# Two small edits in the tail of a decode attention kernel: when the last group's sums are scaled, and how one head's wo rows are loaded

## The chip, the cores and the metric

The kernel runs on one core of a Trainium2 chip. The metric is the device time of one execution in microseconds (us), and the median of several runs is compared. A profile comes from one execution of its own, taken by the hardware profiler; its times count from the start of the profiled span.

## What is computed

Two problems A and B of the same shape stand side by side. Each is one decode step of attention over a sliding window, for a batch of 2 and one query position, followed by the output projection:

```python
B, Sq, D = x.shape                     # 2, 1, 576
Hq, Dh = 32, 128                       # 16 key/value heads, two query heads for each
W = min(4096, max(256, Sk // 4))       # 4096 of 16384 positions
q = (x @ wq) as [B, Hq, Sq, Dh]
k, v = the last W positions of k_cache and v_cache, each head repeated twice
p = softmax(q k^T * Dh ** -0.5)
out = (p v) as [B, Sq, Hq * Dh] @ wo   # wo is [4096, 576]
```

The result is A's and B's output side by side. All inputs are bf16.

## The kernel before

**The work and its order.** The caches dominate: for each problem 16 heads and 2 batch entries of 4096 positions of keys and of values. A step of the main loop handles a *slab*: one key/value head pair of both batch entries, 4 MB of keys (K) and then 4 MB of values (V). There are 16 such steps (`ND`), 8 to a problem, numbered 0 to 15; two steps are a *group* `G` (0 to 7), which shares one block of wo rows. A ring of four 4 MB buffers takes the slabs, in an order written out in `stream`: K of a step comes ahead of V of the step before. At the end it is K15, V13, V14, V15. V15 is loaded in two pieces (`PIECES`), three quarters and one quarter of the positions.

**One step.** VectorE (DVE) transposes K in four parts (`do_X`, `L487`), TensorE (PE) multiplies with the queries into PSUM (`do_S`, `L512`, `L169`), DVE takes the maximum (`do_max`, `L522`), which goes through PE, DVE and ScalarE (ACT) into a bias per row (`do_nm`, `do_nm2`, `do_exp`), and ACT takes the exponential (`L557`), whose sums over the positions come out as one column of `rsum`. DVE transposes the probabilities (`do_pC`, `L565`), and PE multiplies them with V in 32 matmuls (`do_PV`, `L601`). ACT copies that accumulator to SBUF (`L613`). For all groups but the last, GpSimd (POOL) then *folds* it: it masks the copy and adds it together in two halvings (`L620`, `L623`, `L628`), into `acc_r`.

**One group.** `do_tot` does two things before: POOL writes `rsel`, the sums in `rsum` times a mask (`L572`, one instruction), and PE multiplies `rsel` by ones (`tot`, `L575`) so that every row has the totals. DVE takes their reciprocal (`do_rsb`, `L585`). PE brings the folded slabs into place (`do_comb`, `L641`; for the last group `L648`), DVE scales them (`do_norm`), PE and ACT redistribute them (`do_redist`, `L699`, `L707`), and PE multiplies with the group's wo rows (`do_proj`, `L734` with `L169`; for the last group `L738`).

**What sets the order.** Every engine runs its own list of operations in the order in which the program adds them; SP's list holds nearly all DMA issues. An operation's dependencies become waits on semaphores: one counter per engine, one semaphore per DMA buffer. The first waits block all that stands behind them on that engine.

**The tail**, after the main loop (lines 834 to 866), is written out by hand. On PE it runs: V13's products in three parts (rounds 0 to 2, 2 to 4, 4 to 8), with the maximum and the bias of step 15 between them; `tot` of the last group; V14's products (PV14); `comb` of 13 and 14; the redistribution; the projection of group 6 (`proj13`, eight heads); V15's first piece; a redistribution; V15's second piece; `comb` of 15; the projection of step 14 (`proj14`, four heads) and that of step 15 (`proj15`, four heads in three parts, `HEADS`). The fold of slab 13 is added to POOL's list when the last part of V13's products is added; in the kernel before, `rsel` of the last group is added after that.

**The wo rows of the last group.** `issue_wo` loads the four heads of step 14 as one transfer. `issue_last` loads those of step 15 as three: the first two heads (288 KB), the third head (144 KB), the fourth head (144 KB), a head being 128 rows of 1152 bytes, one row to a partition. All are issued from SP behind V15's two pieces. Each of the three parts of `proj15` waits for its own transfer.

Of the kernel before, what the change touches and what calls it, by code (L numbers as in the profile page):

```python
# [59 lines left out]
def build_kernel(nc, probs, out, cfg=None):  # L60
# [28 lines left out]
    HH = HD // 2  # L89
# [8 lines left out]
    BIG = -1.0e30  # L98
    PIECES = [(0, 96), (96, 128)]
    HEADS = [(0, 1), (2,), (3,)]  # L100
    NPC = len(PIECES)

    def by_group(G):
# [3 lines left out]
    with es:  # L107
# [53 lines left out]
        wo_sem = [sem("wo%d" % r) for r in range(2)]  # L161
        x_sem = [sem("xload%d" % P) for P in range(NPROB)]
        wl_sem = [sem("wl%d" % n_) for n_ in range(len(HEADS))]
        out_sem = sem("outdone")
        piece_sem = [sem("piece%d" % n_) for n_ in range(NPC)]

# [10 lines left out]
        def dma_op(eng, sem_h, n_dmas, fn, deps, tag):  # L177
            op = S.add(eng, fn, deps, tag)
            dma_count[sem_h] = dma_count.get(sem_h, 0) + 16 * n_dmas
            op.dma = (sem_h, dma_count[sem_h])  # L180
            return op
# [74 lines left out]

        def issue_last(woP, pc, r0, deps):
            for n_, hs in enumerate(HEADS):
                def f(e, n_=n_, hs=hs):
                    t, r = divmod(hs[0], 2)  # L260
                    row = t * HH + r0 + 256 + 128 * r
                    return e.dma_start(wob[:, pc, 4 + hs[0]:4 + hs[0] + len(hs), :],
                                       woP[row:row + 128 * len(hs), :].rearrange("(h d) n -> d h n", d=128)).then_inc(wl_sem[n_], 16)
                wo_last.append(dma_op("sp", wl_sem[n_], 1, f, deps, "wl%d" % n_))

        def issue_wo(G):
            woP = probs[G // GPP][4]
# [50 lines left out]
        def tb_job(fn, tag, deps, which=None):  # L318
            n = tbn[0]
            tbn[0] += 1  # L320
            w = (tb_last[0] + 1) % NTB if which is None else which
            tb_last[0] = w
            bank = TB[w]
            d = list(deps)
            if tb_open[w] is not None:
                d.append(tb_open[w]())
            tb_open[w] = lambda: tb_consumer[n]
            return n, bank, S.add("pe", lambda e: fn(e, bank), d, tag)
# [236 lines left out]
            chain[(s, "pC")] = S.add("dve", lambda e: e.transpose(  # L565
                pC[:, s % NPT, :, :].rearrange("k j c -> k (j c)"), pR[:, :]), d, "pC%d" % s)

        def do_tot(G):
            d = [chain[(2 * G, "exp")], chain[(2 * G + 1, "exp")], init["maskS"]]
            if G >= 1:  # L570
                d.append(chain[(G - 1, "tot")])
            chain[(G, "rsel")] = S.add("pool", lambda e: e.tensor_tensor(  # L572
                rsel[:, :, :], maskS[:].unsqueeze(1).broadcast_to([128, 2, 8]),
                rsum[:].unsqueeze(2).broadcast_to([128, 2, 8]), ALU.mult), d, "rsel%d" % G)
            n, bank, op = tb_job(lambda e, bank: e.matmul(bank[:, 0:16], ones_f[:, :], rsel[:].rearrange("k l c -> k (l c)"),  # L575
                                                          start=True, stop=True), "tot%d" % G, [chain[(G, "rsel")], p_ones_f])
            chain[(G, "tot")] = op
            chain[(G, "tot_n")] = (n, bank)
# [137 lines left out]
        def do_proj(D_):  # L716
            G = D_ // 2
            P = G // GPP
            pc = G % 2
            new = G % GPP == 0  # L720
            if by_group(G):
                parts = [([(Rsb[:, pc, :, s_], s_) for s_ in range(8)], [r_ev[G]], new, True, True)]
            elif D_ < ND - 1:
                parts = [([(Rsb[:, pc, :, s_], s_) for s_ in range(4)], [r_ev[G], wo_dma[G]] + fin_ops, False, False, False)]
            else:
                parts = [([(oTn[:, h, :], 4 + h) for h in hs], [norm[D_], wo_last[n_]], False, False, n_ == len(HEADS) - 1)
                         for n_, hs in enumerate(HEADS)]
            for lhs, deps, start, rstart, rstop in parts:
                def f(e, rest, lhs=lhs, start=start, rstart=rstart, rstop=rstop):
                    last = None  # L730
                    for n_, (l_, s_) in enumerate(lhs):
                        begin, end = n_ == 0, n_ == len(lhs) - 1
                        if by_group(G):
                            first = e.matmul(OT[0:Bb, 0:NB0], l_, wob[:, pc, s_, 0:NB0], start=start and begin, stop=end, skip_group_check=True)  # L734
                            last = matmul_again(e, first, rest[0:Bb, 0:NB1], wob[:, pc, s_, NB0:NOUT], rstart and begin, rstop and end)
                        else:
                            for half in range(2):
                                last = e.matmul(fin(half), l_, wob[:, pc, s_, half * NH:(half + 1) * NH],  # L738
                                                start=False, stop=end, skip_group_check=True)
                    return last  # L740
                deps = deps + [e_ops[(P - 1, 0)]]
                if by_group(G):
                    n, bank, proj[D_] = tb_job(f, "proj%d" % D_, deps)
                    rest_at[G] = bank
                    if G % GPP < GPP - 1 and G < NG - 2:
                        d = [proj[D_]]
                        if new:
                            if P:
                                d.append(e_ops[(P - 1, 1)])
                            rest_add[G] = S.add("dve", lambda e: e.tensor_copy(o_rest[:, :], bank[0:Bb, 0:NB1]), d, "rest%d" % G)  # L750
                        else:
                            d.append(rest_add[G - 1])
                            rest_add[G] = S.add("dve", lambda e: e.tensor_tensor(o_rest[:, :], o_rest[:, :], bank[0:Bb, 0:NB1], ALU.add),  # L753
                                                d, "rest%d" % G)
                        tb_consumer[n] = rest_add[G]
                    elif G == NG - 2:
                        d = [proj[D_], chain[(ND - 2, "exp")], chain[(ND - 2, "max")]]
                        a_ = S.add("act", lambda e: e.activation(fin(0), OT[0:Bb, 0:NH], ACTF.Copy), d, "fin0")
                        tb_consumer[n] = S.add("dve", lambda e: e.tensor_tensor(
                            fin(1)[:, NB0 - NH:NH], o_rest[:, :], bank[0:Bb, 0:NB1], ALU.add), d + [rest_add[G - 1]], "fin1")  # L760
                        fin_ops.append(S.add("dve", lambda e: e.tensor_copy(fin(1)[:, 0:NB0 - NH], OT[0:Bb, NH:NB0]), [a_], "fin2"))
                    else:
                        rest_at[G] = (n, bank)
                else:
                    proj[D_] = S.add("pe", lambda e, f=f: f(e, None), deps, "proj%d" % D_)
# [27 lines left out]
        for s in range(ND):  # L793
            D2 = s - 2
            c = s - 1
            for u in range(NU):
                if c >= 0:
                    if u == 2:
                        do_nm2(c)
                    elif u == 3:  # L800
                        do_exp(c)
                        if c + 2 < ND:
                            do_fill(c + 2)
                do_X(s, u)
                if c >= 0:
                    if u == 0:
                        do_max(c)
                        if c % 2 == 0 and c >= 2:
                            do_rsb(c // 2 - 1)
                    elif u == 3:  # L810
                        do_pC(c)
                if u >= 1:
                    do_S(s, u - 1)
                if u == 1 and s + 1 < ND:
                    do_zq(s + 1)
                if c >= 0 and u == 1:
                    do_nm(c)
                if D2 >= 0 and D2 % 2 == 1 and s < ND - 1:
                    if u == 2:
                        do_comb(D2)  # L820
                        do_norm(D2)
                    elif u == 3:
                        do_redist(D2 // 2)
            do_S(s, NU - 1)
            if D2 >= 0 and D2 % 2 == 1 and s < ND - 1:
                do_proj(D2)
                if D2 == SPP - 1:
                    do_E(0)
            if c >= 0:
                if c % 2 == 1:  # L830
                    do_tot(c // 2)
                if s < ND - 2:
                    do_PV(c, range(NRD), None)
# [5 lines left out]
        do_nm2(s)  # L839
        do_PV(D_, range(2, 4), None)  # L840
        do_exp(s)
        do_pC(s)
        do_PV(D_, range(4, NRD), None)
        do_tot(s // 2)
# [122 lines left out]
```

## Time and profile before

| | |
|---|---|
| median of 3 runs | 365.75 us |
| lowest and highest of them | 364.33, 365.81 us |
| the profiled execution's own time | 366.16 us |
| its span | 364.8 us |
| read from HBM | 153.10 MB, 420 GB/s over the span |
| busy: PE, DVE, ACT, POOL | 63%, 55%, 19%, 10% of the span |
| granted TensorE clock, mean | 0.85 of full speed |

The profiled execution's own time is its span and what lies around it (launch and end). In the views, `L601` is line 601 of the kernel; `x32` counts instructions. A row of the timeline has start, length, engine, line, operation, the tiles written and read, and in brackets the idle time of the engine just before and what ended it. A row of the windows has busy time and instruction count of PE, PE's weight loads, DVE, ACT and POOL, then the granted clock, the mean busy share of the 16 DMA engines, and GB/s.

### The profile page before, as it was taken

The page shows a single profiled execution, that of the slowest core. Times are in us where ns is not written, and L with a number is a line of the kernel's source. Part 1 is how long each engine was busy: PE and PEld are TensorE (multiplying, and loading weights), DVE is VectorE, ACT ScalarE, POOL GpSimd, SP SyncE. Part 2 cuts the span into 40 slices and gives each one's busy share as a digit, 9 for nine tenths or more (in the row PEclk, how much of TensorE's full clock was granted, in tenths as well). Part 3 has the DMA queues.
Part 4 walks back from the last instruction along what each step waited for, and adds up shares of the span by engine and source line. Part 5 has one row for each costly group of instructions (what it writes and reads, how often), then busy time and mean ns, then how long its engine had stood idle before and what let it go on. Part 6 is the DMA issues. An engine that isn't in the chain of part 4 may idle for free.

```text
span 364.8 us, 2762 instructions
## 1 busy us (share of the span) xinstructions
PE 229.9 (63%) x1323; PEld 59.6 (16%) x954; DVE 201.5 (55%) x176; ACT 68.7 (19%) x153; POOL 35.2 (10%) x55
## 2 busy tenths in 40 slices
PE   0398295576756657573885747594763737576757
PEld 0010021112111211111221201111120201111122
DVE  3013698574908375382917567292926658199631
ACT  1046402020300302020300203120210203021311
POOL 1000000004000130004000040003100040200020
PEclk9999589786996968888786988879896978979968
DMA  8999999999999999999999999999999999999993
GB/s 345 446 417 446 417 408 467 402 446 417 416 438 424 446 417 437 435 428 435 413 444 424 442 419 438 435 428 433 406 446 431 431 429 435 438 428 435 416 413 136
DMA packets 7070, 153.25 MB, mean 420 GB/s; under 512 B 778, under 2 KB 1300, under 8 KB 1684
## 3 DMA queue, kind: packets, MB, share of 16 engines
q1 hardware_dynamic: 7052, 153.10, 98.1%
q8 instruction: 8, 0.13, 0.1%
q14 instruction: 2, 0.02, 0.0%
q10 hardware_dynamic: 8, 0.00, 0.0%
HBM read 153.10 MB, written 0.00 MB: 420 GB/s over the span
## 4 chain that ended last, share of the span: by engine, by line
DMA 63%; DVE 17%; PE 17%; ACT 1%; POOL 1%; issue 1%; SPq 0%; DVEq 0%
DMA ring<-in_B_k_cache_dram 34%; DMA ring<-in_A_k_cache_dram 26%; DVE xt L487 15%; PE st L169 6%; PE st L512 4%; DMA x_sb<-in_B_x_dram 3%; PE acc L601 2%; PE st L423 1%; PE ot L734 1%; PE tb L169 1%; DVE nM L535 1%; DVE m L522 1%; PE ot L169 1%; PE tb L423 1%; PE acc L169 1%
## 5 line engine op out<-in xcount | busy, mean ns | idle before, releaser
L487 DVE STREAM_TRANSPOSE xt<-ring 128x2048 f32<-128x2048 f32 x64 | 145.3, 2285 | 76.0 <-DMA ring<-in_B_k_cache_dram 38.8
L512 PE MATMUL st<-xt,zq 128*128 128x512 bf16 x256 | 116.2, 454 | 112.3 <-DVE xt L487 85.9
L169 PE MATMUL st<-xt,zq 128*128 128x512 bf16 x256 | 114.8, 448 | 0.0
L512 PEld LDWEIGHTS st<-xt,zq 128*128 128x128 bf16 x256 | 28.0, 109 | 207.5 <-DVE xt L487 100.6
L601 PE MATMUL acc<-ring,pC 128*32 128x512 bf16 x512 | 37.4, 408 | 0.0
L540 ACT ACTIVATE nMrep<-nM 1x128 f32<-1x128 f32 x16 | 4.9, 308 | 139.7 <-DVE nM L535 139.7
L613 ACT ACTIVATE acc_sb<-acc 128x512 bf16<-128x512 f32 x16 | 9.5, 596 | 86.6 <-PE acc L601 86.6
L565 DVE STREAM_TRANSPOSE pC<-pR 128x1024 bf16<-128x1024 bf16 x16 | 19.4, 1216 | 4.3 <-ACT pR L557 2.1
L620 POOL TENSOR_TENSOR acc_sb<-acc_sb,maskJ 128x1024 bf16<-128x1024 bf16 (+1 forms) x8 | 13.4, 1679 | 79.3 <-ACT acc_sb L613 79.3
L522 DVE TENSOR_REDUCE m<-st 128x1 f32<-128x1024 f32 x16 | 19.0, 1189 | 1.4 <-PE st L169 1.4
L474 POOL TENSOR_TENSOR zq<-qk,maskA 128x128 bf16<-128x128 bf16 x16 | 6.3, 399 | 125.0 <-PE st L169 103.5
L734 PE MATMUL ot<-wob,Rsb 128*2 128x512 bf16 x56 | 18.0, 439 | 0.3 <-ACT Rsb L707 0.3
L557 ACT ACTIVATE pR<-st,bias_sb 128x1024 bf16<-128x1024 f32 x16 | 17.8, 1114 | 0.5
L447 DVE STREAM_TRANSPOSE qtr<-qrow 128x512 f32<-128x512 f32 x8 | 5.7, 711 | 21.0 <-ACT qrow L437 13.6
L388 ACT ACTIVATE st<-maskB 128x1024 f32<-128x1024 bf16 x16 | 16.5, 1031 | 1.6 <-POOL rsel L572 0.4
L601 PEld LDWEIGHTS acc<-ring,pC 128*32 128x32 bf16 x512 | 13.7, 100 | 14.5 <-issue 4.4
L572 POOL TENSOR_TENSOR rsel<-maskS,rsum 128x16 f32<-128x16 bf16 x8 | 1.7, 216 | 106.9 <-ACT pR L557 106.9
L169 PE MATMUL tb<-wob,Rsb 128*2 128x64 bf16 x56 | 11.7, 209 | 0.0
L355 PE MATMUL tb<-ident_b,x_sb 4*128 4x4 bf16 x4 | 0.3, 174 | 14.2 <-DVE x_dup L362 14.2
L753 DVE TENSOR_TENSOR o_rest<-o_rest,tb 2x64 f32<-2x64 f32 x3 | 0.6, 209 | 15.4 <-PE tb L169 15.4
L623 POOL TENSOR_TENSOR acc_sb<-acc_sb 128x512 bf16<-128x512 bf16 (+1 forms) x8 | 8.2, 1030 | 0.6
L734 PEld LDWEIGHTS ot<-wob,Rsb 128*2 128x2 bf16 x56 | 5.3, 95 | 16.0 <-issue 14.4
(83 smaller groups left out, 107.7 us busy)
## 6 DMA issues: line engine op xcount, KB each, us to landing
ring<-in_A_k_cache_dram SPq DMA_DIRECT2D x8, 4096.0 KB, 31.2
ring<-in_A_v_cache_dram SPq DMA_DIRECT2D x8, 4096.0 KB, 32.4
ring<-in_B_k_cache_dram SPq DMA_DIRECT2D x8, 4096.0 KB, 30.7
ring<-in_B_v_cache_dram SPq DMA_DIRECT2D x7, 4096.0 KB, 32.6
wob<-in_A_wo_dram SPq DMA_DIRECT2D x4, 1152.0 KB, 33.5
ring<-in_A_wq_dram SPq DMA_DIRECT2D x1, 4096.0 KB, 12.6
ring<-in_B_wq_dram SPq DMA_DIRECT2D x1, 4096.0 KB, 22.4
wob<-in_B_wo_dram SPq DMA_DIRECT2D x3, 1152.0 KB, 33.6
```

What stands on the lines that cost most here:

```text
L169: return e.add_instruction(mybir.InstMatmult(name=nc.get_next_instruction_name(), engine=i.engine, ins=[e.lower_ap(rhs), i.ins[1]], outs=[ ...
L388: chain[(s, "fill")] = S.add("act", lambda e: e.activation(ST[s % 2][:, :].rearrange("k (h j) -> k h j", h=2), maskB[:].unsqueeze(1).broad ...
L487: Xop[(s, u)] = S.add("dve", lambda e: e.transpose(xt[:, i % NKT, :].rearrange("k (j w) -> k j w", w=64), ring[:, n % NR, :].bitcast(FP32) ...
L512: first = last = e.matmul(bank, zq[:, p4, s % NZQ, w0:w0 + 128], mv, start=False, stop=stop, skip_group_check=True)
L522: chain[(s, "max")] = S.add("dve", lambda e: e.tensor_reduce(m1[:, 0:1], ST[s % 2][:, :], AX.X, ALU.max), d, "max%d" % s)
L557: chain[(s, "exp")] = S.add("act", lambda e: e.activation(pR[:, :], ST[s % 2][:, :], ACTF.Exp, bias=bias_sb[:, 0:1], scale=SCALE, accum_ou ...
L565: chain[(s, "pC")] = S.add("dve", lambda e: e.transpose(pC[:, s % NPT, :, :].rearrange("k j c -> k (j c)"), pR[:, :]), d, "pC%d" % s)
L601: last = e.matmul(ACC[32 * cb:32 * cb + 32, 0:512], pC[:, D_ % NPT, j0_:j0_ + 4, :].rearrange("k j c -> k (j c)"), ring[:, n % NR, j0_ * 1 ...
L613: acc_ev[D_] = S.add("act", lambda e: e.activation(acc_sb[:, D_ % 2, :], ACC[:, :], ACTF.Copy), d, "accev%d" % D_)
L620: t = S.add("pool", lambda e: e.tensor_tensor(v, v, maskJ[:].unsqueeze(1).unsqueeze(3).broadcast_to([128, l1 - l0, 4, 128]), ALU.mult), [a ...
L623: t = S.add("pool", lambda e: e.tensor_tensor(a_[:, :, 0:256], a_[:, :, 0:256], a_[:, :, 256:512], ALU.add), [t], "acca%d" % D_)
L734: first = e.matmul(OT[0:Bb, 0:NB0], l_, wob[:, pc, s_, 0:NB0], start=start and begin, stop=end, skip_group_check=True)
```

## The change

Two edits, independent of each other.

First, `do_tot` is taken apart. The POOL instruction that writes `rsel` is in a function of its own, `do_rsel`. In the main loop it is called right ahead of `do_tot`; in the tail it is called after `do_exp`, ahead of the last part of V13's products. In POOL's list `rsel` of the last group so stands ahead of the fold of slab 13. `tot` keeps its place on PE.

Second, the third head of step 15 (the second last head) comes by five transfers, of 8, 4, 2, 2 and 112 partitions (`ROWS`), in place of one of 128. Four new semaphores belong to the four small ones. The part of `proj15` that uses this head waits for all five.

```diff
+    ROWS = [(0, 8), (8, 12), (12, 14), (14, 16), (16, 128)]
...
+        part_sem = [sem("part%d" % n_) for n_ in range(len(ROWS) - 1)]
...
         def issue_last(woP, pc, r0, deps):
             for n_, hs in enumerate(HEADS):
...
+                ops = []
+                for i, (d0, d1) in enumerate(ROWS if n_ == 1 else [(0, 128)]):
+                    sem_h = wl_sem[n_] if d1 == 128 else part_sem[i]
+
+                    def f(e, hs=hs, d0=d0, d1=d1, sem_h=sem_h):
+                        t, r = divmod(hs[0], 2)
+                        row = t * HH + r0 + 256 + 128 * r
+                        return e.dma_start(wob[d0:d1, pc, 4 + hs[0]:4 + hs[0] + len(hs), :],
+                                           woP[row:row + 128 * len(hs), :].rearrange("(h d) n -> d h n", d=128)[d0:d1]).then_inc(sem_h, 16)
+                    ops.append(dma_op("sp", sem_h, 1, f, deps, "wl%d_%d" % (n_, i)))
+                wo_last.append(ops)
...
-        def do_tot(G):
+        def do_rsel(G):
             d = [chain[(2 * G, "exp")], chain[(2 * G + 1, "exp")], init["maskS"]]
...
+        def do_tot(G):
             n, bank, op = tb_job(lambda e, bank: e.matmul(bank[:, 0:16], ones_f[:, :], rsel[:].rearrange("k l c -> k (l c)"),
...
-                parts = [([(oTn[:, h, :], 4 + h) for h in hs], [norm[D_], wo_last[n_]], False, False, n_ == len(HEADS) - 1)
+                parts = [([(oTn[:, h, :], 4 + h) for h in hs], [norm[D_]] + wo_last[n_], False, False, n_ == len(HEADS) - 1)
...
                 if c % 2 == 1:
+                    do_rsel(c // 2)
                     do_tot(c // 2)
...
         do_exp(s)
+        do_rsel(s // 2)
         do_pC(s)
         do_PV(D_, range(4, NRD), None)
         do_tot(s // 2)
```

More of the change, by code (lines that the diff above doesn't have):

```diff
@@ L258, in issue_last @@
             for n_, hs in enumerate(HEADS):
[L259 to L264, printed above, removed]
+                ops = []
[8 more added lines that the diff above has]
+                wo_last.append(ops)
         def issue_wo(G):
```

## The prediction

> **What bounds the kernel now.** I read the page first: the span, and the DMA row of its 40 slices.
>
> ```profile
> span 364.8 us, 2762 instructions
> DMA  8999999999999999999999999999999999999993
> ```
>
> The transfers run without a gap until the last slice, so upstream nothing but bytes counts, and this change moves none of them. What is open is the tail. The second view is the chain of work that ended last, in order of time; its columns are start, length and engine with line.
>
> ```profile
> 346.53 0.50 ACT acc_sb L613
> 347.10 1.05 POOL acc_sb L620
> ...
> 348.96 0.42 POOL acc_r L628
> ...
> 360.38 0.57 PE acc L601 x8
> ...
> 361.89 1.09 PE st L738 x16
> 363.01 0.45 DVE out_sb L771
> ```
>
> From 346.5 on no transfer stands in it. The last slab's exponential ends at 346.53, GpSimd (POOL) folds the third last slab (`L620` to `L628`), and what follows is on TensorE (PE), VectorE and ScalarE (ACT) up to the last copy of the output at 363.01. The timeline tells where PE sat still:
>
> ```profile
> 345.02 1.05 PE L601 MATMUL acc<-ring,pC 128*32 128x512 bf16 x16
> 349.34 0.22 POOL L572 TENSOR_TENSOR rsel<-maskS,rsum 128x16 f32<-128x16 bf16 x1
> 349.61 0.61 PE L575 MATMUL tb<-rsel,ones_f 128*128 128x16 f32 x2 [3.55 <-POOL rsel L572]
> 350.15 3.60 PE L601 MATMUL acc<-ring,pC 128*32 128x512 bf16 x32
> 355.18 0.59 PE L734 MATMUL ot<-wob,Rsb 128*2 128x512 bf16 x1 [0.27 <-ACT Rsb L707]
> ```
>
> PE waited 3.55 us for `rsel`, which stood behind the fold on POOL, though its own input was there at 346.53. The second last slab's 32 products (PV14) stood behind `tot` (`L575`) on PE.
>
> The third view is when data lands: start of the issue on the SP queue, and time from issue to landing.
>
> ```profile
> 314.87 0.53 SPq L241 DMA_DIRECT2D ring<-in_B_v_cache_dram  x1
> ring<-in_B_v_cache_dram SPq DMA_DIRECT2D x1, 4096.0 KB, 32.6
> 329.29 1.18 SPq L237 DMA_DIRECT2D ring<-in_B_v_cache_dram  x2
> ring<-in_B_v_cache_dram SPq DMA_DIRECT2D x1, 3072.0 KB, 25.5
> ring<-in_B_v_cache_dram SPq DMA_DIRECT2D x1, 1024.0 KB, 27.4
> L262 SPq DMA_DIRECT2D wob<-in_B_wo_dram x3: 432/467/596, 331.2 to 332.3; - x3
> DMA to landing us min/median/max: 27.8/28.1/28.3
> ```
>
> V14 lands at 314.87 + 32.6 = 347.5. The last slab's pieces land at 329.3 + 25.5 = 354.8 and, issued half of 1.18 us later, at 329.9 + 27.4 = 357.3. The three wo transfers of the last heads, issued from 331.2 to 332.3, land at 331.2 + 28.3 = 359.5, about 359.8, and 332.3 + 27.8 = 360.1; the 576 KB of the other heads, queued ahead of them, before that. So before, all bytes are there at 360.1 and PE ends near 363.0: the tail is PE's, by some 2.5 us.
>
> The fourth view explains why PE is so late: 3.41 us windows, with PE busy time first and the granted clock (PEclk) after POOL.
>
> ```profile
> 222.05:225.47 3.42, 1.43 (x10) 0.42 (x5) 3.33 (x2) 1.44 (x4) 0.00 (x0) 1.00 1.06 452
> 225.47:228.88 3.41, 3.41 (x8) 0.50 (x4) 0.00 (x0) 0.00 (x0) 0.00 (x0) 0.50 1.05 452
> 245.95:249.36 3.41, 1.62 (x8) 0.47 (x5) 1.29 (x2) 0.45 (x1) 0.00 (x0) 1.00 1.05 452
> 249.36:252.77 3.41, 2.25 (x36) 1.04 (x34) 0.00 (x0) 0.60 (x1) 0.43 (x1) 1.00 1.03 442
> 256.19:259.60 3.41, 2.71 (x7) 0.54 (x4) 3.41 (x4) 0.00 (x0) 0.37 (x2) 0.50 1.05 452
> 259.60:263.01 3.41, 2.91 (x16) 0.89 (x9) 3.38 (x6) 0.81 (x3) 0.00 (x0) 1.00 0.89 382
> 344.93:348.35 3.42, 1.14 (x17) 0.41 (x17) 1.25 (x1) 1.86 (x4) 1.17 (x2) 1.00 0.97 414
> 348.35:351.76 3.41, 2.15 (x18) 1.11 (x22) 0.26 (x1) 0.00 (x0) 1.13 (x3) 0.50 1.04 447
> 351.76:355.17 3.41, 2.59 (x28) 0.92 (x20) 1.03 (x5) 0.78 (x2) 0.00 (x0) 0.50 0.88 371
> 355.17:358.59 3.42, 3.41 (x21) 1.02 (x14) 0.22 (x1) 0.00 (x0) 0.00 (x0) 0.50 0.94 364
> 358.59:362.00 3.41, 2.71 (x46) 1.08 (x38) 0.69 (x3) 1.14 (x3) 0.00 (x0) 1.00 0.15 54
> ```
>
> Each pair shows one step of the clock. A full-clock window with 1.43 us busy is followed by 0.50; one with 1.62 by 1.00. A half-clock window with 2.59 is followed by 0.50; one with 2.71 by 1.00. The 3.55 us wait left 1.14 us in its window, and PE then ran at half clock for 10.2 us, through PV14 and the eight-head projection of the group before last (`proj13`).
>
> [...]
>
> **The change, part 1: `rsel` ahead of the fold.** Nothing is added; one 0.22 us POOL instruction changes its place. For the other seven groups `do_rsel` and `do_tot` are still called one after the other, so nothing moves there. In the tail `rsel` can start at about 346.6 and ends by 346.85. The fold behind it on POOL starts at 347.10, when ACT has copied the accumulator, so it is not delayed. The added wait on POOL (for the last exponential) has only this fold behind it, and that waits longer.
>
> Step by step, with the windows where they lay before. `tot` starts at 346.9 instead of 349.61 and takes under 0.6 us, so PE is at PV14 by 347.5, when V14 lands: the wait that was removed gives way to a DMA, 2.6 us sooner. The window to 348.35 now holds 1.05 + 0.5 + 0.85 = 2.4 us of PE work, above 1.62: the clock stays at 1.00. At full clock the same work is in the trace:
>
> ```profile
> 291.01 1.91 PE L601 MATMUL acc<-ring,pC 128*32 128x512 bf16 x32
> 310.96 0.38 PE L734 MATMUL ot<-wob,Rsb 128*2 128x512 bf16 x1
> 312.89 0.19 PE L169 MATMUL tb<-wob,Rsb 128*2 128x64 bf16 x1
> L738 PE MATMUL st<-wob,oTn x8: 285/286/286, 362.3 to 362.7; 128*2 128x288 bf16 x8
> ```
>
> PV14 then takes 1.9 us, not 3.6, to 349.4. The fold is ready at 348.96 + 0.42 = 349.4, so both inputs of the next step come together. From the end of PV14 to `proj13` it was 355.18 - 353.75 = 1.4 us: `proj13` starts at 350.9 and needs 312.89 - 310.96, some 2.0 us: 352.9. PE then waits for the first piece (354.8), takes 24 of 32 products, 1.4 us, to 356.2, and waits for the second (357.3). From that piece's first product to the fourth head's matmuls, the last ones (`L738`), it was 362.7 - 360.4 = 2.3 us: 359.6. But that head's rows land at 360.1. The tail becomes a DMA's: last matmuls at 360.15, 0.29 us long, and `out_sb` at 360.5 instead of 363.01. **The saving is 2.5 us**, and PE has 0.5 us of cover before it would be late again.
>
> **Part 2: the split of one 144 KB transfer into five.** SP issues four DMAs more, each 0.43 to 0.6 us by the `L262` row, 1.9 us in all. The last head's issue moves from 332.3 to 334.2, 24 us before its data comes, so behind the queued slabs this costs nothing; also behind it is only the store of the first problem's output, due at the very end. If the queue were empty it would cost the 1.9 us. PE has four semaphores more to wait for ahead of the third head, while it waits for data anyway.
>
> A transfer of a few partitions behind a full queue isn't in the trace, so I bound its landing. The 16 DMA engines moved 447 GB/s from 348.35 to 351.76 (the row above), 27.9 each, and a row of wo has 1152 bytes: 0.041 us. At best each late engine has one row less: -0.04 us. At worst all 16 split rows fall to the last engine: 0.66 us, less that 0.04: +0.62. The engines do not end together:
>
> ```profile
> 359.00:360.00 1.00, 1.00 (x18) 0.40 (x10) 0.60 (x2) 0.35 (x1) 0.00 (x0) 1.00 0.30 104
> ```
>
> In the last us before 360 their mean busy share is 0.30, so most have room for rows; I take 0.
>
> **The sum.** The profiled run took 366.16, 0.41 above the median of 365.75, with a span of 364.8 and 1.36 around it. Its own new time is 366.16 - 2.5 = 363.66; from the median it is 363.25. I take the middle, **363.4**.
>
> **Rivals.**
>
> (A) *The clock falls in the new wait for the last slab.* PE now has holes from 352.9 to 354.8 and from 356.2 to 357.3. With the old windows, 351.76 to 355.17 holds about 1.1 + 0.4 us, between the 1.43 and 1.62 of the rows; the next holds 1.6 at full clock, or some 3 at half clock, and either lets the last stage run at 1.00. If the windows lie 0.2 us or more later, the one that ends near 358.8 holds under 1.43 at full clock, or under 2.59 at half: from there PE is at half clock. Then all PE work of the last stage takes twice as long: the second piece's 8 products 0.45 us more, the four small products before the norm 0.2, the 14 matmuls ahead of the last pair 0.9 (`L738`, 16 in 1.09), so that the last pair starts at 359.6 + 1.55 = 361.2, takes 0.45, and the output is copied at 361.7 instead of 363.01: the saving is 1.3 and the time 364.4. For it speaks how close the sums are; against it that the two upper runs of before (365.75, 365.81), near the profiled one, suggest windows that lie alike.
>
> [...] In before's three runs a second level shows once at most (364.33).
>
> (B) *The split pays a completion for each small transfer, in a row.* The nearest row is the wait of SP for the output store:
>
> ```profile
> SPq L928 <- DMA out_dram<-out_sb: 1.0, 1, 1.0
> ```
>
> Four times 1.0 us on the engines that serve the few partitions lands the last rows at 364.1, 4.0 later than counted: 4.0 - 2.5 = 1.5 us slower, 367.2. It decides from 0.62 us for each. Against it: the three wo transfers of before land 0.3 us apart, and 147 KB at 447 GB/s are 0.33 us, so a completion shows no price of its own there.
>
> [...]
>
> (C) *Nothing gained*: `tot` goes early, but PV14 is held by something else until about 350. Then the time stays within 0.5 us of 365.7. Against it: the chain names only `rsel`, and V14's landing is read off.
>
> **How the numbers follow.** Forecast 0.55, A 0.34, B 0.05, C 0.06. Half a per cent, 1.83 us, is about what a measurement can tell from no change. The forecast lies beyond it, A and C within it; B is slower by 0.4% at its price, beyond 0.5% only if dearer. Faster 0.55, same 0.42, slower 0.03. The range: below, the saving from the median with 0.04 for the rows and 0.4 for the difference between runs, 362.8; above, A counted from the profiled run, 366.16 - 1.3 = 364.9, with half of the split's 0.62, 365.2; B and most of C are left out.
>
> **What would show it.** Right: `tot` near 346.9 with `rsel` ahead of `L620`; PV14 at 347.5, released by a DMA, in 1.9 us; PEclk 1.00 where it was 0.50; the last projection released by a wo landing near 360.1. Wrong: PEclk 0.50 after 358.6 (A); a wo landing after 361 (B); PV14 still near 350 (C).

## The result, and the profile after

The changed kernel takes **363.54 us** (median of 15 runs, 363.14 to 365.27); the kernel before, beside it, 365.81 us (15 runs, 364.33 to 366.59). The ratio is 0.9951, 95% interval 0.9934 to 0.9967. The medians differ by 2.27 us; 2.5 and a time of 363.4 were forecast. The profiled execution of the changed kernel took 363.54 us, with a span of 362.3 (before: 366.16 and 364.8).

The timeline of the tail, changed kernel, laid out as before:

```profile
346.23 0.22 POOL L579 TENSOR_TENSOR rsel<-maskS,rsum 128x16 f32<-128x16 bf16 x1 [18.32 <-ACT pR L564]
346.50 0.40 PE L584 MATMUL tb<-rsel,ones_f 128*128 128x16 f32 x2 [0.82 <-POOL rsel L579]
346.72 1.04 POOL L629 TENSOR_TENSOR acc_sb<-acc_sb,maskJ 128x512 bf16<-128x512 bf16 x1 [0.27 <-ACT acc_sb L622]
347.00 1.91 PE L610 MATMUL acc<-ring,pC 128*32 128x512 bf16 x32
...
350.54 0.38 PE L743 MATMUL ot<-wob,Rsb 128*2 128x512 bf16 x1 [0.27 <-DVE om L696]
...
354.30 1.48 PE L610 MATMUL acc<-ring,pC 128*32 128x512 bf16 x24 [1.64 <-DMA ring<-in_B_v_cache_dram]
356.79 0.61 PE L610 MATMUL acc<-ring,pC 128*32 128x512 bf16 x8 [0.88 <-DMA ring<-in_B_v_cache_dram]
358.46 1.06 PE L747 MATMUL st<-wob,Rsb 128*2 128x288 bf16 x8
359.34 1.13 PE L747 MATMUL st<-wob,oTn 128*2 128x288 bf16 x8
360.52 0.45 DVE L780 CAST out_sb<-st 2x288 bf16<-2x288 f32 x1 [1.95 <-PE st L747]
```

`rsel` now runs ahead of the fold (`L629`), and PE waits 0.82 us for it instead of 3.55. PV14 starts at 347.00 instead of 350.15 and takes 1.91 us instead of 3.60; `proj13` starts at 350.54 instead of 355.18. PE then waits for the two pieces of the last slab (the two DMA rows), where before it came late to both. `out_sb` starts at 360.52 instead of 363.01.

The chain that ended last, its last three steps:

```profile
330.00 28.42 DMA wob<-in_B_wo_dram
358.46 2.04 PE st L747 x16
360.52 0.45 DVE out_sb L780
```

A transfer stands in the tail of the chain, where it was `rsel`, the fold and PE before. It is that of step 14's four heads, landing at 358.42. Behind it PE doesn't wait again: the 16 last matmuls take 2.04 us, where before they took 1.09, so that the last rows (359.74) are there before PE comes to them. The windows (3.41 us each: in this trace and in before's every stretch of one granted clock that ends inside the span lasts a whole number of them, 3.41 to 34.13 us; granted clock behind POOL's column) say why:

```profile
344.90:348.32 3.42, 2.50 (x46) 1.15 (x42) 1.39 (x2) 1.71 (x4) 1.74 (x3) 1.00 1.02 436
348.32:351.73 3.41, 2.44 (x29) 0.90 (x17) 1.16 (x5) 0.78 (x2) 0.61 (x2) 1.00 0.94 404
351.73:355.14 3.41, 1.77 (x24) 0.70 (x23) 0.61 (x2) 0.36 (x1) 0.00 (x0) 1.00 0.96 402
355.14:358.56 3.42, 1.75 (x28) 0.60 (x22) 0.16 (x1) 0.78 (x2) 0.00 (x0) 1.00 0.91 335
358.56:361.97 3.41, 1.92 (x16) 0.63 (x12) 0.46 (x2) 0.40 (x1) 0.00 (x0) 0.50 0.13 44
```

The half clock that PE had from 348.35 to 358.59 is gone, and a new one begins at 358.56, in the last stage. That is rival A's mechanism, and the sign that the prediction gave for it (PEclk 0.50 after 358.6). How little it cost follows below.

When data lands, from the trace's DMA records (each the last landing of its kind):

| | before | after |
|---|---|---|
| V14 | 347.48 | 346.95 |
| V15's two pieces | 354.79, 357.29 | 354.26, 356.75 |
| wo of step 15: first two heads, third head, fourth head | 359.42, 359.79, 360.16 | 359.21, 359.48, 359.74 |

In this run the stream of transfers is ahead of before's, by 0.5 us for V14 and the two pieces and by 0.2 to 0.4 for the wo rows. The edits can't be the reason: V14 was issued near 314.6, and the first instructions that they touch are SP's added issues, after 331. From the second piece to the last wo landing it is 2.87 us before and 2.99 after: with the split the rows land no sooner.

### The profile page after: what moved, and what is told of

The parts are those of the page before. It is cut to its first block, busy times and chain, and to the rows that moved or that the text cites. A ratio compares the mean times of both kernels' runs of the same rounds, so it can differ in the third digit from the quotient of the medians.

```text
span 362.3 us, 2770 instructions
## 1 busy us (share of the span) xinstructions
PE 228.3 (63%) x1324; PEld 58.8 (16%) x954; DVE 201.7 (56%) x176; ACT 68.8 (19%) x153; POOL 35.4 (10%) x55
## 4 chain that ended last, share of the span: by engine, by line
DMA 71%; DVE 14%; PE 14%; SPq 1%; issue 0%; ACT 0%; DVEq 0%
DMA ring<-in_B_k_cache_dram 34%; DMA ring<-in_A_k_cache_dram 26%; DVE xt L494 13%; DMA wob<-in_B_wo_dram 8%; PE st L171 5%; PE st L519 4%; DMA x_sb<-in_B_x_dram 3%; PE st L430 1%; PE ot L171 1%; PE acc L171 1%; PE tb L171 1%; PE tb L430 1%; PE st L747 1%; DVE nM L542 1%; PE tb L532 0%
## 5 line engine op out<-in xcount | busy, mean ns | idle before, releaser
L610 PE MATMUL acc<-ring,pC 128*32 128x512 bf16 x512 | 34.9, 390 | 2.6 <-DMA ring<-in_B_v_cache_dram 2.5
L629 POOL TENSOR_TENSOR acc_sb<-acc_sb,maskJ 128x1024 bf16<-128x1024 bf16 (+1 forms) x8 | 13.4, 1681 | 60.6 <-ACT acc_sb L622 60.6
L743 PE MATMUL ot<-wob,Rsb 128*2 128x512 bf16 x56 | 15.9, 402 | 0.3 <-DVE om L696 0.3
L542 DVE TENSOR_REDUCE nM<-tb 1x8 f32<-1x128 f32 x16 | 4.4, 273 | 6.4 <-PE tb L532 6.4
```

What stands on the lines that cost most here:

```text
L610: last = e.matmul(ACC[32 * cb:32 * cb + 32, 0:512], pC[:, D_ % NPT, j0_:j0_ + 4, :].rearrange("k j c -> k (j c)"), ring[:, n % NR, j0_ * 1 ...
L629: t = S.add("pool", lambda e: e.tensor_tensor(v, v, maskJ[:].unsqueeze(1).unsqueeze(3).broadcast_to([128, l1 - l0, 4, 128]), ALU.mult), [a ...
```

## The experiments

Two theories were tried against each other. **T1**: the gain is the removed wait for `rsel`, with the half clock that the wait caused. **T2**, the rival: the split of the transfer makes the rows land earlier and brings part or all of the gain. A second question was which half of T1 costs the time, the wait or the clock. Each kernel ran beside the kernel before on the same chip; the medians of before were 366.01 (e1 to e4), 366.25 (e5 to e8) and 365.87 (e9 to e12). What lies around the span varies from 1.2 to 3.1 us between runs, so where tenths matter the spans are compared. All ratios are to the kernel before.

**e1: the first edit alone.**

```
-    ROWS = [(0, 8), (8, 12), (12, 14), (14, 16), (16, 128)]
+    ROWS = [(0, 128)]
```

> The first edit alone: rsel early, the third head in one transfer of 128 partitions. Theory 1 (the whole gain comes from rsel): 363.5 us, within 0.3 of the changed kernel, ratio near 0.994, tot at about 346.5 to 346.9 and PV14 right when V14 lands. Theory 2 (the split brings a share, because the late DMA engines get fewer rows): 364.0 us or more, and the last wo landing 0.3 us or more later after V15's second piece than in the changed kernel.

Measured: 363.68 us (6 runs), ratio 0.9942 (0.992 to 0.9964), median span 361.9. **The whole gain is in the first edit**; T2 falls. The last wo landing comes 2.86 us after the second piece, sooner than the changed kernel's 2.99. Its windows and PV14's row of the timeline:

```profile
344.11:347.52 3.41, 2.00 (x31) 0.99 (x31) 1.39 (x2) 2.01 (x5) 1.20 (x2) 1.00 1.01 432
347.52:350.94 3.42, 3.05 (x34) 0.98 (x22) 0.30 (x3) 0.47 (x1) 1.16 (x3) 0.50 0.95 410
350.94:354.35 3.41, 2.57 (x22) 0.95 (x14) 1.18 (x4) 0.66 (x3) 0.00 (x0) 1.00 0.94 399
```

```profile
347.14 3.28 PE L610 MATMUL acc<-ring,pC 128*32 128x512 bf16 x32 [0.43 <-DMA ring<-in_B_v_cache_dram]
```

In this run the windows lie elsewhere (borders at 347.52 and 350.94, not at 348.35 and 351.76), and PV14 runs at half clock although the wait is gone: 3.28 us. It cost nothing, since PE waits for the last slab afterwards: `out_sb` starts at 360.12, 0.37 us after the last wo landing (359.75). So full clock in PV14, a step of the forecast, isn't needed for the gain.

**e2: the second edit alone.** `rsel` goes back behind the last products:

```
-        do_rsel(s // 2)
         do_pC(s)
         do_PV(D_, range(4, NRD), None)
+        do_rsel(s // 2)
         do_tot(s // 2)
```

> The second edit alone: five transfers for the third head, rsel behind the fold as before. Theory 1: the same as before, 365.8 us, ratio 1.000 within 0.002, with PE still waiting 3.5 us for rsel. Theory 2: at least 0.5 us faster than before. Rival (each small transfer pays a completion of its own): the last wo landing up to 4 us later, and slower by up to 1.5 us.

Measured: 366.14 us (12 runs), ratio 1.0004 (0.9989 to 1.0019). The split alone gives nothing and costs nothing. Its profiled run is one of the shorter ones, span 363.1, with the same wait. The timeline, then the windows:

```profile
349.94 0.61 PE L584 MATMUL tb<-rsel,ones_f 128*128 128x16 f32 x2 [3.55 <-POOL rsel L579]
```

```profile
346.47:349.88 3.41, 0.00 (x0) 0.00 (x0) 1.25 (x1) 0.88 (x3) 2.30 (x4) 1.00 0.94 404
349.88:353.30 3.42, 3.36 (x30) 1.58 (x34) 0.26 (x1) 0.00 (x0) 0.01 (x1) 0.50 0.98 417
353.30:356.71 3.41, 2.56 (x32) 1.00 (x18) 1.26 (x5) 0.78 (x2) 0.00 (x0) 1.00 0.98 398
```

The window lies on the wait almost exactly, so PE is at half clock for one window only and not for three: the wait is as long as before's, 3.55 us, and the span is 1.7 us shorter than before's profiled one. That points at the clock rather than at the wait.

**e3: the wait is kept, the clock isn't let down.** Neither edit; in the wait PE multiplies constants into a free PSUM bank, and nobody reads the result.

```
+        def warm(n_mm, tag):
+            ...
+                for _ in range(n_mm):
+                    last = e.matmul(bank[:, 0:512], ones_b[:, :], maskB[:, :], start=True, stop=True)
...
+        warm(13, "warm_a")
         do_tot(s // 2)
```

> The kernel before, with neither edit, but with 13 matmuls of constants (their result is never used) on PE in the wait for rsel, some 2.8 us, into a PSUM bank that is free then. tot still starts near 349.6. Theory 1a (what the wait cost was the half clock after it, not its 3.5 us): the clock stays at 1.00, PV14 takes 1.9 us, the projection of eight heads 2.0, the tail is bound by the landings, and the time is 363.5 to 363.9 us. Theory 1b (the wait itself is what was lost): 365.3 to 365.8 us.

Measured: 364.58 us (12 runs), ratio 0.9967 (0.9955 to 0.9978). From its timeline:

```profile
346.74 2.98 PE L343 MATMUL tb<-maskB,ones_b 128*128 128x512 bf16 x13
...
350.37 0.40 PE L596 MATMUL tb<-rsel,ones_f 128*128 128x16 f32 x2 [0.64 <-POOL rsel L591]
350.69 1.91 PE L622 MATMUL acc<-ring,pC 128*32 128x512 bf16 x32
...
360.93 1.12 PE L759 MATMUL st<-wob,oTn 128*2 128x288 bf16 x8 [1.27 <-DMA wob<-in_B_wo_dram]
```

`tot` is even later than before (350.37 for 349.61), PV14 is back at 1.91 us, and PE waits for wo at the end (the clock falls only in that wait, at 360.50). The gain was smaller than the changed kernel's (spans 363.1 to 363.8), and the time missed both expected ranges. A wo transfer of 128 partitions lands in 16 parts in the traces; the last part of the last rows came at 361.52, the other 15 by 359.88. The trace has an instruction fetch at 358.44: 16 KB of the program's own code, about 1.07 us long. The records don't name a packet's engine; that the late part and the fetch share one is read from their times. The page counts these fetches among the queues. First before, then after:

```profile
q8 instruction: 8, 0.13, 0.1%
```

```profile
q8 instruction: 9, 0.15, 0.2%
```

**e4: the changed kernel with PE kept busy in the tail**, by 6, 3 and 3 such matmuls ahead of the two pieces and of the norm.

```
+        warm(6, "warm_b")
         do_PV(D_, range(PIECES[0]...
+        warm(3, "warm_c")
         do_PV(D_, range(PIECES[1][0]...
+        warm(3, "warm_d")
         do_comb(D_)
```

> The changed kernel with 6, 3 and 3 matmuls of constants (result never used) in PE's waits for V15's first piece, for its second piece, and for the copy of the last accumulator. Theory (in the changed kernel's profile PEclk fell to 0.50 at 358.56 and the last 16 matmuls took 2.04 us; at full clock the last landing binds): out_sb 0.4 us sooner, 363.1 us, and the slowest runs (364 to 365) gone. Rival (the landings bind anyway): 363.5 us as before, or slower by 0.2 if the added matmuls delay a product.

Measured: 364.82 us (12 runs), ratio 0.997 (0.9957 to 0.9983). This missed: it is slower than the changed kernel (its 12 spans are 363.3 to 363.7, those of the changed kernel 361.9 to 363.4), although the last stage ran at full clock. The timeline, and the queues from 358.1 to 358.6 us:

```profile
358.43 0.66 PE L759 MATMUL st<-wob,Rsb 128*2 128x288 bf16 x8
...
360.75 0.88 PE L759 MATMUL st<-wob,oTn 128*2 128x288 bf16 x8 [1.66 <-DMA wob<-in_B_wo_dram]
```

```profile
q1 hardware_dynamic: 105, 0.11, 61.5%
q8 instruction: 1, 0.02, 13.2%
```

13.2% of 16 engines over 0.5 us are 1.06 us of one engine. Again one part of 16 of each of the last three wo transfers is late (the last at 361.30, the other parts by 359.73), as if the ninth fetch fell on an engine that still had wo rows to move. PE waits 1.66 us.

**e5: e3 with fewer PE instructions.** The constants are loaded once, and `rsel` and `tot` go in bf16.

```
-                    last = e.matmul(bank[:, 0:512], ones_b[:, :], maskB[:, :], start=True, stop=True)
+                    last = matmul_again(e, first, bank[:, 0:cols], maskB[:, 0:cols], True, True, False)
...
-        rsel = sb("rsel", [128, 2, 8], FP32)
+        rsel = sb("rsel", [128, 2, 8], BF16)
```

> As e3 (neither edit, 13 matmuls of constants in the wait for rsel), but with fewer PE instructions: the constants are loaded as weights once, and rsel is bf16, so that each tot is one pass and not two. New theory (e3 and e4 lost 1.3 us because their 24 PE instructions more brought a ninth 16 KB fetch of instructions, at 358.4, onto a DMA engine that still had wo rows to bring): eight fetches, last wo landing near 359.8, 363.5 us, so that the half clock alone accounts for all 2.3 us between the kernels. Rival (the wait itself costs a part): 364.4 us or more, with the same eight fetches.

Measured: 363.98 us (363.19, 363.47, 364.48, 364.75), ratio 0.9938 (0.9917 to 0.996). From the timeline of its profiled run:

```profile
349.42 0.18 PE L596 MATMUL tb<-rsel,ones_b 128*128 128x16 bf16 x1 [0.64 <-POOL rsel L591]
349.53 1.91 PE L622 MATMUL acc<-ring,pC 128*32 128x512 bf16 x32
...
356.78 0.61 PE L622 MATMUL acc<-ring,pC 128*32 128x512 bf16 x8 [0.39 <-DMA ring<-in_B_v_cache_dram]
```

The windows over the wait and behind it:

```profile
345.00:348.40 3.40, 3.24 (x28) 0.31 (x9) 1.25 (x1) 1.79 (x4) 1.42 (x2) 1.00 1.04 448
348.40:351.80 3.40, 2.54 (x37) 0.97 (x35) 0.44 (x3) 0.31 (x1) 0.88 (x3) 1.00 0.90 386
351.80:355.20 3.40, 2.78 (x36) 1.25 (x32) 1.26 (x5) 0.67 (x3) 0.00 (x0) 1.00 0.97 408
```

`tot` is nearly as late as before (349.42 for 349.61), yet PE is in time for the last slab's second piece and waits 0.39 us for it. The bf16 `tot` is itself some 0.2 us shorter than a two-pass one at full clock (0.18 for 0.40), less than that wait. **With the clock held, the wait for `rsel` fits into the waits for data that come after it.** The expected eight fetches didn't come about: the profiled run (364.48, span 363.1) had a ninth at 358.34, and one late part in the last two wo transfers (361.00, the other parts by 359.60), as in e3. The two runs with spans of 361.9 and 362.1 took 363.19 and 363.47, the time of the first edit.

**e6: the best version that the runs suggested**: first edit, no split, the lean constants (5, 3 and 3), bf16 `rsel`.

> The first edit alone with 5, 3 and 3 matmuls of constants in PE's last three waits and a bf16 rsel, about as many PE instructions as before. Fetch theory: eight fetches, PEclk 1.00 to the end in every phase of the windows, out_sb 0.35 us after the last wo landing: 363.1 us, and no run above 363.8. Rival (the matmuls themselves delayed e4): 364.5 us again.

Measured: 363.39 us (4 runs), ratio 0.9922 (0.9907 to 0.9937), spans 361.8 to 362.2, eight fetches. The last two windows:

```profile
355.20:358.60 3.40, 3.17 (x40) 0.69 (x28) 0.00 (x0) 0.77 (x2) 0.00 (x0) 1.00 0.91 350
358.60:362.00 3.40, 1.60 (x20) 0.61 (x19) 0.61 (x2) 0.40 (x1) 0.00 (x0) 1.00 0.12 43
```

The last stage is at full clock, and `out_sb` starts at 360.36.

**e7: does the number of PE instructions bring the ninth fetch?** First edit, and 24 tiny matmuls early in the kernel.

```
+                if s == 4 and u == 0:
+                    warm(24, "extra", 32)
                 do_X(s, u)
```

> The first edit alone with 24 tiny matmuls of constants (32 columns) in the fifth step of the main loop, where PE waits for keys; the tail is untouched. Fetch theory: a ninth fetch of instructions in the tail; where it meets a DMA engine with wo rows to bring, the last landing is 1 to 1.5 us later: 364.5 to 365 us. Rival (only work in the tail matters): 363.6 us, as e1.

Measured: 363.31 us (363.3, 363.3, 363.32, 364.82), ratio 0.993 (0.9909 to 0.9952). Mostly a miss: the ninth fetch came, at 359.12, but delayed no wo rows in the profiled run, and only one of four spans (363.5) is long.

**e8: the changed kernel, one semaphore for the five transfers.**

```
-                    sem_h = wl_sem[n_] if d1 == 128 else part_sem[i]
+                    sem_h = wl_sem[n_]
```

> Both edits, with one semaphore for the five transfers of the third head in place of five, so that PE has one wait in place of five. Theory (the split neither costs nor brings): the five small issues stay, and it is 363.5 us as the changed kernel, with eight fetches and not nine. Rival (the four waits or the ninth fetch cost the changed kernel something): 363.2 us, and no runs above 364.

Measured: 363.5 us (4 runs), ratio 0.9928 (0.9911 to 0.9944). The four further waits cost nothing that shows. The expected eight fetches were nine again, at 359.25 and harmless.

**e9: sixteen transfers of one partition and one of 112**, one semaphore, to make the price of a small transfer visible.

```
-    ROWS = [(0, 8), (8, 12), (12, 14), (14, 16), (16, 128)]
+    ROWS = [(i, i + 1) for i in range(16)] + [(16, 128)]
```

> Both edits, with the third head's first 16 rows in 16 transfers of one partition in place of four transfers, and one semaphore for all 17. Theory (a small transfer behind the full queue has no price of its own beyond its bytes): the last wo landing 3.0 to 3.1 us after V15's second piece, as in the changed kernel, 363.5 us. Rival (each pays a completion of 0.6 to 1.0 us on its DMA engine): the last landing 8 us later or more, 370 us or more.

Measured: 364.25 us (7 runs), ratio 0.9965 (0.9945 to 0.9986), median span 362.9 against 362.25 in e8 (on another chip; 362.5 for the changed kernel in e11, on the same one). The chain's end, and the issues with the time from issue to landing:

```profile
348.62 11.90 DMA wob<-in_B_wo_dram
360.57 0.66 PE st L747 x4
361.25 0.45 DVE out_sb L780
```

```profile
L268 SPq DMA_DIRECT2D wob<-in_B_wo_dram x19: 246/596/2385, 330.9 to 349.5; - x19
...
DMA to landing us min/median/max: 11.2/33.7/35.6
```

By the trace's records the last one-partition transfers land evenly, 0.18 us apart, which I read as one engine's pace. A row's bytes are 0.04 us of that (1152 bytes at 27.9 GB/s): a small transfer pays some 0.14 us there. The last landing comes 3.74 us after the second piece, in e8 2.98. So neither side of the dispute had it: 1.0 us each (rival B) is refuted, nothing at all is too. SP's 19 issues are also drawn out to 349.5, one of them taking 2.39 us.

The change's own split has a small price too. From the second piece to the last wo landing it is 2.98 to 3.06 us with it (the changed kernel, e2, e8, e10) and 2.85 to 2.92 without (before, e1, e6, e7, e12), in the profiled runs that have no late part: about 0.1 us, too little to show in the times.

**e10: the changed kernel with bf16 `rsel`** (fewer PE instructions, as in e5).

> Both edits, with rsel in bf16, so that each of the eight tot is one pass: 16 PE instructions fewer than the changed kernel. Theory (the ninth fetch of instructions costs 1.3 us in the runs where it meets a busy DMA engine): eight fetches, 363.4 us, and no span above 363. Rival (the runs of the changed kernel above 364 come from something else): a few of them here too.

Measured: 363.67 us (6 runs), ratio 0.9946 (0.9926 to 0.9966), spans 361.8 to 362.5. The ninth fetch came at 363.6, after the span. No span is above 363, but two times are above 364 (364.47 and 364.97, spans 361.8 and 362.4): so some of the times above 364 come from what lies around the span, as the rival had it.

**e11 and e12: the changed kernel and e6's kernel again, on one chip.**

> The changed kernel as it is, on the same chip as the others of this call: 363.6 us, nine fetches in its profile, some runs at 364.5 or above.

> The kernel of e6 again (first edit, bf16 rsel, 5, 3 and 3 matmuls of constants in PE's last waits), next to the changed kernel on the same chip. Theory: full clock in the tail and eight fetches make it 0.2 to 0.4 us faster than the changed kernel: 363.3 us, all runs below 364. Rival: equal within 0.1 us.

Measured: e11 363.94 us (12 runs), ratio 0.9953 (0.9934 to 0.9972), spans 362.0 to 363.7, median 362.5. e12 363.59 us (6 runs), ratio 0.9939 (0.992 to 0.9957), all spans 361.8 to 362.0, though two times are above 364, against what was expected. e11's profiled run is one of three with a span above 363.4. The chain, and the queues from 358.1 to 358.6 us:

```profile
330.81 29.84 DMA wob<-in_B_wo_dram
360.78 1.14 PE st L747 x8
361.95 0.45 DVE out_sb L780
```

```profile
q8 instruction: 1, 0.02, 13.6%
```

The transfer in the chain is that of step 15's first two heads, landing at 360.65. Again a fetch (358.20) goes with one late part in each of the last three wo transfers: the last rows land at 361.34, their other parts by 359.92. e12's kernel has 0.6 us less median span than the changed one, and no long span; in the time, the two intervals overlap.

## Why the prediction was right

Before is 365.8, the forecast 363.4, the result 363.5. Point by point, by the prediction's own steps:

- **`rsel` and `tot` go early, and the fold isn't delayed**: right. Both, like V14's landing, are 0.4 to 0.5 us earlier than said (`tot` 346.50 for 346.9), about as much as that run's transfers were ahead.
- **PV14 is released by V14's landing and runs at full clock in 1.9 us**: right in this run. e1 shows that the full clock there isn't needed: at half clock, 3.28 us, PE was still in time (in e10's profiled run too, 3.49 us).
- **"The saving is 2.5 us", from the wait and its clock**: right in size, and e1 and e2 put it on the first edit. The shares can be told now:

| | wait for `rsel` | half-clock windows behind it | `out_sb` starts |
|---|---|---|---|
| before | 3.55 us | three | 363.01 |
| e2 | 3.55 us | one | 361.34 |
| e5, run with a fetch in the tail | as long, filled with constants | none | 361.37 |
| e1 | none | one | 360.12 |
| changed | none | none until 358.56 | 360.52 |

  e5's row holds the delay of the late part; its two shorter runs, which I take to be without one, have e1's span, 361.9 to 362.1. So in these runs the late `tot` by itself cost nothing measurable; before, it cost through the half-clock windows behind it. The prediction had both in one sum and didn't part them.
- **PE waits for the pieces, then for the last head's rows**: right for the pieces (354.30 and 356.79), wrong for the rows in the profiled run. There PE waits 0.18 us for step 14's heads and then, at half clock, never again; the last rows lie ready from 359.74. The sign given for being right, a last projection released by a wo landing near 360.1, is not in this run. It is in e1's: its last two matmuls start at 359.79, behind the landing at 359.75.
- **Rival A, "from there PE is at half clock", a price of 1.3 us**: the mechanism came, the size was off. Two steps failed. First the condition: with the windows lying as before (358.56 here, 358.59 there) it was to stay away, since the window ahead of the last held 1.6 us, near a window with 1.62 that kept the clock. Here 1.75 us lost it, and in e1 2.00 us. The changed kernel's own window before it kept the clock with 1.77 (24 matmuls). So busy time in that column isn't by itself what decides. In the main loop it sorts the windows well: in the 14 profiled runs each full-clock window below 1.42 us lost the clock and each above 1.44 kept it (in before's and the changed kernel's, the highest that lost it held 1.43 us and the lowest that kept it 1.49). In the tail some with 1.64 to 2.00 lost it and others with 1.70 to 1.87 kept it. The 8 matmuls of the 1.62 window were of the form `128*128`; of the 28 and 31 most were of the form `128*32` (20 of the 28), and such matmuls overlap: PV14's 32, of 0.38 us each, took 1.91 us. What is weighed instead stays open. Second the price: A let the second piece's products and the norm run at half clock too (1.55 us more in all), although by its own schedule those products start at 357.3, ahead of the 358.8 from which it let the clock fall. The clock fell only after them, so only the last 16 matmuls were doubled, 2.04 us for 1.09, and about half of the added time would have been a wait for the last rows at full clock. What reached the end is about 0.4 us: `out_sb` starts 0.78 us after the last landing (359.74), where the prediction had counted 0.35 (360.15 to 360.5).
- **The two errors cancel**: the transfers of this run ended 0.4 us sooner than before's (359.74 for 360.16), and the clock took 0.4 us back. Before's landing was the odd one: in the other profiled runs without a late part and without e9's small transfers it is 359.57 to 359.99. `out_sb` at 360.52 for a forecast of 360.5 is therefore partly luck; the 2.3 us between the medians are not.
- **The split at 0, bounds -0.04 to +0.62**: right for this kernel (e2: 1.0004; e1 against the changed kernel: no difference that the intervals show). The upper bound counted bytes alone; e9 shows 0.14 us more for each transfer on its engine, and the landings show a price of about 0.1 us for the split as it is. SP's issues of the split took about 0.3 us each, where 0.43 to 0.6 were counted.
- **Rival B, 1.0 us for each small transfer**: refuted by e9; even sixteen in place of four cost 0.76 us together at the landing (3.74 against 2.98). For one row, 0.14 of its 0.18 us are not its bytes, by the estimate from e9, but a size like that doesn't show in the time here (ratio 0.9928 in e8, 0.9942 in e1 without the split).
- **Rival C**: refuted by PV14 at 347.00.
- **Where the windows lie in another run**, left open in rival A ("If the windows lie 0.2 us or more later"): elsewhere in two runs. The borders fell at 347.52 in e1 and 349.88 in e2, and at 348.32 and 348.35 in the changed kernel's and before's profiled runs; what sets their place isn't shown. Windows that lie differently also fit the second level of before's times (364.33 to 364.37 in 4 of 15 runs): e2's profiled run, with the same wait, has one half-clock window and a span of 363.1. That these runs of before had such windows was not seen in a trace of theirs.

**What stays open**: what decides whether the ninth fetch comes before, among or after the last rows. Fewer PE instructions went with eight in the span in the profiled runs of e1, e6 and e10, but e12, the same kernel as e6, had it at 359.28, and e5 and e8 had nine where eight were expected. That the fetch makes the long spans is read from four profiled runs (e3, e4, e5, e11): in each a fetch starts between 358.20 and 358.44, and one part of the last rows is late. In the profiled runs where the ninth fetch starts at 359.12 or later, no part is late by as much. No run varied the fetch alone. What the clock weighs in the windows of the tail is open as well.

## What to carry to other kernels

A wait ahead of a stage that waits for data anyway cost little by itself here (e5: `tot` at 349.42, two spans of 361.9 and 362.1, where e1's median without the wait is 361.9); ask first what it does to the clock in the windows behind it, and price those. Windows lay differently in the profiled runs (borders at 347.52, 348.32, 348.35 and 349.88), so a margin of some tenths in one profile decides nothing: count the cases. The busy time of a window of one kind of matmul didn't tell what a window of another kind needs: 1.62 us of `128*128` kept the clock, 1.75 and 2.00 us of mostly `128*32` lost it. When the tail becomes a transfer's, look at everything else that moves by DMA then, the program's own code too (16 KB in 1.06 us among the last wo rows, in e4).

## What was not expected of the hardware

- **Code fetches appear to share the DMA engines with the data.** The program is fetched in pieces of 16 KB, 8 or 9 in a span, each one packet, of 0.93 to 1.11 us in before's and the changed kernel's traces. Where one started at 358.2 to 358.5, among the last wo rows, one part of these landed 1.4 to 1.6 us behind the others (e4 361.30 for 359.73, e11 361.34 for 359.92); where it started at 359.1 or later, no such delay is seen.
- **In this tail the waits for data hid either the late `tot` or a half-clock window, not both**: e1 hides a half-clock window, e5 hides the late `tot`. Before's profiled run had the late `tot` with three such windows, e2's with one, and their `out_sb` starts 2.9 and 1.2 us after e1's.
- **A one-partition transfer behind a full queue** took about 0.18 us of its engine, an estimate from the even landings of e9; 0.04 of it are the bytes (1152 at 27.9 GB/s, a sixteenth of before's 447 from 348.35 to 351.76).
